# An attention block and two mixture-of-experts layers on one core: the first expert's row list and row evictions rearranged

## The chip, the cores and the metric

The kernel runs on one core of one Trainium2 chip. The metric is the device time of one execution in microseconds (us); lower is better. Five engines work on their own instruction streams, each in order: TensorE (PE in the profile, its weight loads PEld), VectorE (DVE), ScalarE (ACT), GpSimd (POOL) and SyncE (SP), which here only issues DMAs. Semaphores tie them together. On-chip memory is SBUF; TensorE writes to PSUM.

## The reference, cut to what matters

Attention over 4 batches, 8 heads, 768 positions in chunks of 32 gives `x`, 3072 rows of 512. Then come two layers of 8 experts with `relu(x @ w1[e]) @ w2[e]`:

```python
# layer 1: greedy assignment, each token to one expert, each expert takes 3072/8 = 384 tokens
logits = x @ w_gate
for idx in np.argsort(-logits.flatten()):
    tok, e = idx // E, idx % E
    if assigned[tok] >= 0 or counts[e] >= cap: continue
    assigned[tok] = e; counts[e] += 1
out[mask_e] = relu(x[mask_e] @ w1[e]) @ w2[e]
# layer 2: top 2 of 8 of noisy logits, weighted sum of the two experts
out[mask] += top2_w[mask, k, None] * (relu(x[mask] @ w1[e]) @ w2[e])
```

The change lies between attention and the first expert of layer 1.

## The kernel before, in words

**Attention** (`attention`) works on 24 tiles of 128 tokens and stores each row to DRAM (`xr`) as two f16 halves, high and low part, plus some columns of metadata. Constants are converted on POOL during attention, two of `ctx.chores` per tile (`setup`).

**Layer 1's assignment** (`route`) is done expert by expert: k = 0 to 7 are turns, and in each turn one expert fills up. A turn first proposes for each token its best open expert (`propose`: V, eq, mx, OH), then searches the threshold in several steps (GE on VectorE, counts on TensorE, `rps`), then names the expert (`m8`, and `est`, which the weight loads on SP's queue read) and the tokens that are sure. The second turn (k = 1) waits at line 782 before it starts on its steps.

**The list** (`lists1`, `slot_list`) turns a mask of tokens into a list of row numbers: each token's slot number is split into low bits (`bi`, 32 values) and high bits (`ai`, 12 values); `oa` is a one-hot of the high bits, `r` is `oa` times the token's number, `oh` (in the trace `sloh`) a one-hot of the low bits, [tokens of a partition 24, 32], made in steps of 512 elements. 24 small products with `oh[:, c]` as weights and `r[:, c]` as moving operand (`slps`) give the list in PSUM, 32 partitions x 12. Four evictions on VectorE (`idx`) lay it out on 128 partitions.

**The gather** (`gather1`) issues three indirect DMAs on POOL for the 384 rows of an expert. For experts 0 and 1, `transpose` transposes each tile of 128 rows on TensorE into one PSUM tile (`tps`, 8 blocks of 128, f16; the pool has two buffers), and one ScalarE operation evicts it to `xT`. For the others a transposing DMA does it. Then come `mm1` (products `m`) and for experts 0 to 4 `mm2_f32` (products `m2f`).

**The order of the instructions** is not left to the engines: the program keeps its own books (class `Pipe`) of when each engine would be free and each tile ready, and runs some twenty generators (loads, lists, gathers, splits of weights, routing) that each yield the time, in the books, at which their next instructions are due. TensorE's clock in the books drives them. While TensorE has nothing due, `until` writes one small product on ones (a filler, in the trace `m<-ones`) into its queue and advances the clock by its book time, 128 / 2.4 + 3 = 56.3 ns. What is written stays written: on the chip each engine runs its queue in order.

The weights of an expert are split into a high and a low f16 part (`split`, `halves`): the high part on ScalarE, the residual `w_..l` on VectorE or, for expert 0, also on POOL when it is idle in the books. The second turn's start (lines 778 to 783) asks for expert 0's first pair of `w1` tiles.

The lines of the books that matter here (`account`, 123 to 135, and `wait`, 195); `e` is the engine, `g` POOL:

```python
        elif e == "v":
            rate = 0.52 if op in ("tensor_scalar", "tensor_copy") and not ps else 6.25 if op == "reciprocal" else 1.04
            cost = 69.0 + 60.0 * ptr + rate * n
        elif e == "s":
            cost = (51.0 if ps else 93.0) + 94.0 * (ptr or "accum_out" in kw) + 0.833 * n
        else:
            cost = 147.0 + 1.887 * n if op == "tensor_tensor" else (245.0 if ptr else 122.0) + 0.832 * n

        if op in ("tensor_tensor", "scalar_tensor_tensor") and not ps:
            if e == "g":
                if self.t["v"] > start:
                    start += 200.0
                    self.t["v"] += cost
...
        self.until(lambda: self.rdy("p", *aps) <= self.t["p"] + 60.0, spare)
```

`ps` says that an operand lies in PSUM, `n` is the number of elements in a partition, `rdy` adds about 0.2 us for the way from engine to engine. `mm1` calls `pipe.wait(*w1, xT, spare=ps)` (line 1205) ahead of an expert's first product.

Of the kernel before, what the change touches and what calls it, by code (L numbers as in the profile page):

```python
# [9 lines left out]
F16 = mybir.dt.float16  # L10
BF16 = mybir.dt.bfloat16
I32 = mybir.dt.int32
AF = mybir.ActivationFunctionType
ALU = mybir.AluOpType
# [10 lines left out]
NTOK, DM, E, FF = B * S, H * D, 8, 1024  # L25
KT, FT = DM // 128, FF // 128
G = NTOK // 128
# [585 lines left out]
def slot_list(ctx, pi, na, low, ids, late=0.0):  # L613

    pipe, pool = ctx.pipe, ctx.rt
    V_, P_ = pipe.V, pipe.P
    ni, nc_ = ids.shape[2], ids.shape[1]  # L620

    def tl(n, shape, dt):
        return pool.tile(shape, dt, tag=f"sl{n}", name=f"sl{n}")

    bi, ai = (tl(n, [128, nc_], I32) for n in ("bi", "ai"))
    V_.tensor_scalar(bi, pi, low - 1, None, op0=ALU.bitwise_and)
    V_.tensor_scalar(ai, pi, low.bit_length() - 1, None, op0=ALU.arith_shift_right)
    yield pipe.t["v"] - 100
    oa = tl("oa", [128, nc_, na], F16)
    V_.tensor_tensor(  # L630
        oa, ai.unsqueeze(2).to_broadcast([128, nc_, na]),
        ctx.cols[low][:, :na].unsqueeze(1).to_broadcast([128, nc_, na]), op=ALU.is_equal,
    )
    yield pipe.t["v"] - 100
    r = tl("r", [128, nc_, na, ni], F16)
    V_.tensor_tensor(
        r, oa.unsqueeze(3).to_broadcast([128, nc_, na, ni]), ids.unsqueeze(2).to_broadcast([128, nc_, na, ni]),
        op=ALU.mult,
    )
    oh = tl("oh", [128, nc_, low], F16)  # L640
    step = 512 // low
    for c in range(0, nc_, step):
        yield pipe.t["v"] - 100
        cs = slice(c, min(c + step, nc_))
        m = cs.stop - cs.start
        V_.tensor_tensor(
            oh[:, cs], ctx.iota16[:, :low].unsqueeze(1).to_broadcast([128, m, low]),
            bi[:, cs].unsqueeze(2).to_broadcast([128, m, low]), op=ALU.is_equal,
        )
    ctx.spread += 1  # L650
    yield pipe.rdy("p", oh, r) + late
    yield from lock(ctx)
    ps = ctx.ms.tile([low, na, ni], F32, tag="msl", name="slps")
    for c in range(nc_):
        P_.matmul(
            ps.rearrange("p a b -> p (a b)"), oh[:, c], r[:, c].rearrange("p a b -> p (a b)"),
            start=(c == 0), stop=(c == nc_ - 1),
        )
    yield pipe.rdy("v", ps) - (0 if late else 200)
    return ps  # L660


def lists1(ctx):

    pipe, pool = ctx.pipe, ctx.rt
    V_ = pipe.V
    for k in range(E):
        yield lambda: k in ctx.sure
        mk = ctx.sure[k]
        ps = yield from positions(ctx, mk.unsqueeze(1), "l1")  # L670
        yield lambda: k in ctx.closed
        pos = ps[:, 0]
        if ctx.closed[k] is not None:
            at, before = ctx.closed[k]
            pos = pool.tile([128, G], F32, tag="lpos", name=f"lpos{k}")
            V_.tensor_tensor(pos, ps[:, 0], before, op=ALU.add)
            V_.tensor_tensor(mk, mk, at, op=ALU.add)
        na = CAP // 128
        pi = pool.tile([128, G], I32, tag="slpi", name="slpi")
        V_.scalar_tensor_tensor(pi, mk, -FAR, pos, op0=ALU.mult, op1=ALU.add)  # L680
        unlock(ctx)
        ps = yield from slot_list(ctx, pi, 4 * na, 32, ctx.tokid)
        for q in range(4):
            V_.tensor_scalar(
                ctx.idx1[32 * q : 32 * q + 32, k], ps[:, :, 0].rearrange("p (a q) -> p q a", q=4)[:, q],
                float(NTOK // 2), None, op0=ALU.add,
            )
        unlock(ctx)
        ctx.listed.add(k)


def route(ctx):
# [7 lines left out]
    pipe, pool = ctx.pipe, ctx.rt  # L700
    V_, P_ = pipe.V, pipe.P
# [27 lines left out]
    for k in range(E):  # L729
        def tl(shape, dt, n, **kw):  # L730
            return pool.tile(shape, dt, tag="rt" + n, name=f"{n}_{k}", **kw)
# [7 lines left out]
        def est():  # L739
            V_.tensor_scalar(ctx.est[:, k : k + 1], m8[:1], -1.0, float(E), op0=ALU.mult, op1=ALU.add)  # L740
            ctx.est_known.add(k)
# [36 lines left out]
        if k:  # L778
            s0, cand = 0, ctx.cand0
            if k == 1:  # L780

                yield lambda: k - 1 in ctx.listed and 0 in ctx.W and ctx.W[0]["w1"]
            *_, (V, OH, mx) = prop
        else:
            s0 = 2
            V, OH, mx = ctx.V0, ctx.OH0, ctx.mx0
            dg = pst([128, E])
            P_.matmul(dg, ctx.onesb[:NH], ctx.flh, start=True, stop=True)
            dgh = tl([128, E], F32, "dgh")
            V_.tensor_copy(dgh, dg)  # L790
            dg = dgh
            tables = top(dg, plan.shifts[1], slice(off[1], off[2]), slice(off[2], off[-1] + 1))
            next(tables)
            next(tables)
            cand = R[:, off[1] :].bitcast(F32)
        for s in range(s0, NS):
            nj, o = plan.nj[s], off[s]
            GE = tl([128, G * NJ], F16, "GE")[:, : G * nj].rearrange("p (c j) -> p c j", j=nj)
            step = G if k else G // 2
# [90 lines left out]
        V_.scalar_tensor_tensor(fl8, score, smax, ctx.e8f, op0=ALU.is_equal, op1=ALU.mult)  # L890
        V_.tensor_scalar(above, V, tf, None, op0=ALU.is_gt)
        V_.tensor_reduce(m8, fl8, axis=AX.X, op=ALU.max)
        inc, exc = tl([128, G], F32, "inc"), tl([128, G], F16, "exc")
        ind, bE = tl([128, E], F32, "ind"), tl([128, E], F32, "bE")
        cs, slack = tl([128, E], F32, "cs"), tl([128, E], F32, "slack")
# [4 lines left out]
        for i in range(0, G, G // 4):  # L900
            P_.matmul(cg, ctx.ones16, NQ[:, :, i : i + G // 4], start=(i == 0), stop=(i == G - G // 4))
        V_.scalar_tensor_tensor(at, mx, m8, at, op0=ALU.is_equal, op1=ALU.mult)
        est()
        V_.tensor_scalar(bE, ctx.e8f, m8, -2.0 * BIG, op0=ALU.is_equal, op1=ALU.mult)
        V_.tensor_tensor_scan(inc, ctx.keep[:, 0], at, 0.0, op0=ALU.mult, op1=ALU.add)
        V_.tensor_reduce(cs, cg, axis=AX.X, op=ALU.add)
# [373 lines left out]
    return ps  # L1280


def transpose(ctx, xT, rows, tile_):

    pipe = ctx.pipe
    yield pipe.rdy("p", tile_)
    ps = ctx.m2.tile([128, 2 * KT, 128], F16, tag="m2", name="tps")
    for kt in range(2 * KT):
        pipe.P.transpose(ps[:, kt], rows[:, 128 * kt : 128 * kt + 128], ctx.id16)
    pipe.S.activation(xT, ps, AF.Copy)  # L1290


def gather1(ctx, k):
# [5 lines left out]
    xg = []  # L1299
# [14 lines left out]
    for a in range(NA):  # L1314
        rows = xg[a][:, :DM].bitcast(F16)
        if k > 1:
            yield pipe.rdy("y", xg[a])
            pipe.D.dma_start_transpose(xT[:, :, 128 * a : 128 * a + 128], rows)
        else:
            yield from transpose(ctx, xT[:, :, 128 * a : 128 * a + 128], rows, xg[a])  # L1320
    ctx.X1[k] = (xT, ix)
    for a in range(NA):
        pipe.G.tensor_copy(ix[:, a : a + 1], xg[a][:, DM : DM + 1])
# [558 lines left out]
def setup(ctx, cp):  # L1882
# [9 lines left out]
    def half(n, src, dt=F16):  # L1892
        tl = cp.tile(list(src.shape), dt, name=n)
        nc.gpsimd.tensor_copy(tl, src)
        setattr(ctx, n, tl)
# [48 lines left out]
    def cols(low):  # L1944
        half(f"cols{low}", getattr(ctx, f"cols{low}"))
        ctx.cols[low] = getattr(ctx, f"cols{low}")


    ctx.chores = [
        lambda: half("e8", ctx.e8f),  # L1950
        lambda: half("tri16", ctx.tri),
        lambda: half("iota16", ctx.iota),
        lambda: half("tokid", ctx.tokid),
        lambda: half("slotid", ctx.slotid),
        lambda: cols(32),
# [67 lines left out]
```

## Time and profile before

| | |
|---|---|
| time, median of 3 runs | 1055.89 us (1055.35 to 1056.14) |
| the profiled execution | 1053.0 us, its span 1051.2 us |
| busy PE / DVE / ACT / POOL | 986.2 / 642.3 / 461.8 / 296.0 us |
| mean granted TensorE clock | 0.976 |
| end of attention, first turn of routing, list | up to 152.6 us |
| first gather issued | 152.87 us |
| first product of expert 0 | 162.45 us |

Times in rows are microseconds from the start of the span. A row of a timeline has start, duration, engine, line, operation, output <- inputs, shape and count, and in square brackets the idle time ahead of it with what ended it. Line 68 is that of a helper through which all instructions behind attention pass, so rows are told apart by their tiles.

### The profile page before, as it was taken

How to read it: one execution, taken by the hardware profiler on the slowest of the kernel's cores; microseconds unless marked ns; L12 is line 12 of the kernel's file. 1: busy time of each engine (PE TensorE's matmuls, PEld its weight loads, DVE VectorE, ACT ScalarE, POOL GpSimd, SP SyncE). 2: the span in 40 equal slices, each digit the busy share in tenths (PEclk: the TensorE clock that was granted, in tenths of full speed). 3: DMA queues.
4: the chain of work that ended last, by engine and by line, in shares of the span. 5: the costliest groups of instructions: out<-in, count | busy, mean ns of one | idle time of the engine just before them, and what ended most of it. 6: DMA issues, size and time to landing. Idle time of an engine off the chain costs nothing.

```text
span 1051.2 us, 21987 instructions
## 1 busy us (share of the span) xinstructions
PE 986.2 (94%) x8312; PEld 592.7 (56%) x8312; DVE 642.3 (61%) x2096; ACT 461.8 (44%) x817; POOL 296.0 (28%) x471
## 2 busy tenths in 40 slices
PE   7787649999999999998989999999999999999997
PEld 4676546767676676544555454455555555555553
DVE  6687775666666758695774846545455454564221
ACT  2576514444534446986506535245153351533110
POOL 6565414101102023101021323333233331232321
PEclk9899859999999999999999999999999999999999
DMA  8898833557578486959349748539367393664520
GB/s 238 255 267 235 304 137 123 186 159 210 169 225 203 151 203 192 305 165 201 62 105 268 241 133 244 140 106 260 95 203 176 88 286 87 167 116 110 115 66 31
DMA packets 147253, 184.61 MB, mean 176 GB/s; under 512 B 105558, under 2 KB 106070, under 8 KB 145608
## 3 DMA queue, kind: packets, MB, share of 16 engines
q1 hardware_dynamic: 129814, 131.74, 46.2%
q0 software_dynamic: 13872, 45.15, 14.7%
q10 hardware_dynamic: 3458, 6.30, 1.7%
q8 instruction: 66, 1.08, 0.5%
q14 instruction: 43, 0.35, 0.1%
HBM read 127.10 MB, written 32.44 MB: 152 GB/s over the span
## 4 chain that ended last, share of the span: by engine, by line
PE 71%; DMA 11%; DVE 6%; issue 5%; ACT 3%; SPq 2%; POOL 1%; ACTq 0%; POOLq 0%; DVEq 0%
PE m L68 55%; PE m2f L68 10%; DMA v<-vctx_dram 4%; PE rps L68 3%; DMA k<-kT_dram 1%; DMA yT<-rb 1%; SPq L280 1%; DMA xg<-xr,idx 1%; ACT junk L68 1%; SPq L278 1%; DMA xr<-rb 1%; PE slps L68 1%; PE sb L304 1%; DVE sloh L68 1%; DMA st<-x_dram 1%
## 5 line engine op out<-in xcount | busy, mean ns | idle before, releaser
L68 PEld LDWEIGHTS <-hT 128*128 128x128 f16 (+2 forms) x1800 | 143.5, 99 | 159.5 <-issue 5.1
L68 ACT ACTIVATE hT<-m 128x384 f16<-128x384 f32 (+2 forms) x152 | 75.6, 499 | 274.6 <-PE m L68 271.6
L68 DVE SCALAR_TENSOR_TENSOR hT<-m,hT 128x384 f16<-128x384 f32 (+2 forms) x152 | 86.4, 569 | 96.3 <-ACT hT L68 96.2
L68 ACT ACTIVATE junk<-st 128x1024 f16<-128x1024 f32 x108 | 113.6, 1052 | 61.4 <-DMA st<-x_dram 26.0
L68 PE MATMUL m2f<-st,hT 128*128 128x256 f32 x480 | 127.6, 398 | 0.6 <-ACT hT L68 0.6
L68 POOL DMA_INDIRECT out_dram<-pv,ts x47 | 48.9, 1040 | 257.5 <-DVE pv L68 99.3
L68 DVE SCALAR_TENSOR_TENSOR pv<-m,ys,pv 128x512 f32<-128x512 f32 (+2 forms) x47 | 33.5, 714 | 118.8 <-PE m L68 118.7
L68 PE MATMUL m<-xT,w_0h 128*128 128x384 f16 (+2 forms) x384 | 96.6, 331 | 2.8 <-DMA xT<-xg 2.8
L68 PE MATMUL m<-xT,w_2h 128*128 128x384 f16 (+2 forms) x384 | 96.7, 331 | 1.7 <-DVE hT L68 1.7
L68 PE MATMUL m<-xT,w_1h 128*128 128x384 f16 (+2 forms) x384 | 96.5, 331 | 0.0
L68 PE MATMUL m<-xT,w_3h 128*128 128x384 f16 (+2 forms) x384 | 96.4, 331 | 0.0
L68 PEld LDWEIGHTS m2f<-st,hT 128*128 128x128 f32 x480 | 83.4, 190 | 10.2 <-ACT hT L68 1.0
L68 PE MATMUL m<-w_3h,hT 128*128 128x512 f16 (+2 forms) x300 | 71.6, 345 | 1.4 <-DVE hT L68 1.4
L68 PE MATMUL m<-w_0h,hT 128*128 128x512 f16 (+2 forms) x300 | 72.7, 348 | 0.0
L68 PE MATMUL m<-w_1h,hT 128*128 128x512 f16 (+2 forms) x300 | 72.1, 347 | 0.0
L68 PE MATMUL m<-w_2h,hT 128*128 128x512 f16 (+2 forms) x300 | 71.5, 345 | 0.0
L68 PE MATMUL m<-xT,w_2l 128*128 128x384 f16 (+2 forms) x192 | 63.6, 331 | 0.0
L68 PE MATMUL m<-xT,w_1l 128*128 128x384 f16 (+2 forms) x192 | 63.6, 331 | 0.0
L68 PE MATMUL m<-xT,w_3l 128*128 128x384 f16 (+2 forms) x192 | 63.6, 331 | 0.0
L68 PE MATMUL m<-xT,w_0l 128*128 128x384 f16 (+2 forms) x192 | 63.6, 331 | 0.0
L68 POOL DMA_INDIRECT xg<-x,rows x54 | 53.2, 985 | 29.9 <-issue 11.7
L68 POOL DMA_INDIRECT xg<-xr,idx x24 | 25.0, 1040 | 129.1 <-DVE idx L68 39.0
(336 smaller groups left out, 1870.2 us busy)
## 6 DMA issues: line engine op xcount, KB each, us to landing
st<-w_dram SPq DMA_DIRECT2D x64, 512.0 KB
st<-x_dram SPq DMA_DIRECT2D x64, 512.0 KB
xr<-rb SPq DMA_DIRECT2D x24, 264.0 KB
x<-rb SPq DMA_DIRECT2D x24, 264.0 KB
v<-vctx_dram SPq DMA_DIRECT2D x12, 520.0 KB
v<-vctx_dram SPq DMA_DIRECT2D x24, 260.0 KB
q<-qT_dram SPq DMA_DIRECT2D x12, 512.0 KB
out_dram<-zero ACTq DMA_DIRECT2D x24, 256.0 KB
```

The costliest lines, as they stand in the source:

```text
L68: return f(*args, **kw)
L278: nc.sync.dma_start(behind[:, n : n + 1], flown[-AHEAD])
L280: nc.sync.dma_start(out, src)
L304: nc.tensor.matmul(sc[CH * c : CH * c + CH, hp], q[:, hp, CH * o : CH * o + CH], k[:, :, hp, k0 : k0 + KEYS], start=True, stop=True,)
```

## The change

- In `slot_list` with 32 low values, the low bits are converted to f16 (`bw`, then a copy), the one-hot becomes [32, 24], tokens innermost, in one operation against a new constant `ctx.lows`, and the weights of product c are `oh[:, :, c]`. This holds for the eight lists of layer 1.
- `lows` is one more chore on POOL, in fourth place.
- In `lists1`, for the first expert, index evictions 1 and 3 of four go to ScalarE.
- In `route`, `est` of the first turn is written directly behind `m8` instead of behind the products that follow; the second turn waits for expert 0's gathers to be issued instead of for its list.
- `transpose` for expert 0 evicts the first half of the columns on ScalarE and the second on VectorE.

```diff
@@ slot_list
-    bi, ai = (tl(n, [128, nc_], I32) for n in ("bi", "ai"))
-    V_.tensor_scalar(bi, pi, low - 1, None, op0=ALU.bitwise_and)
-    V_.tensor_scalar(ai, pi, low.bit_length() - 1, None, op0=ALU.arith_shift_right)
+    bi, ai = tl("bi", [128, nc_], F16 if low < 128 else I32), tl("ai", [128, nc_], I32)
+    if low < 128:
+        bw = tl("bw", [128, nc_], I32)
+        V_.tensor_scalar(bw, pi, low - 1, None, op0=ALU.bitwise_and)
+        V_.tensor_scalar(ai, pi, low.bit_length() - 1, None, op0=ALU.arith_shift_right)
+        V_.tensor_copy(bi, bw)
...
-    oh = tl("oh", [128, nc_, low], F16)
+    if low < 128:
+        yield pipe.t["v"] - 100
+        oh = tl("oh", [128, low, nc_], F16)
+        V_.tensor_tensor(oh, ctx.lows, bi.unsqueeze(1).to_broadcast([128, low, nc_]), op=ALU.is_equal)
+        hot = lambda c: oh[:, :, c]
+    else:
+        oh = tl("oh", [128, nc_, low], F16)
+        hot = lambda c: oh[:, c]
...
-            ps.rearrange("p a b -> p (a b)"), oh[:, c], r[:, c].rearrange("p a b -> p (a b)"),
+            ps.rearrange("p a b -> p (a b)"), hot(c), r[:, c].rearrange("p a b -> p (a b)"),
@@ lists1
-            V_.tensor_scalar(
-                ctx.idx1[32 * q : 32 * q + 32, k], ps[:, :, 0].rearrange("p (a q) -> p q a", q=4)[:, q],
-                float(NTOK // 2), None, op0=ALU.add,
-            )
+            out, src = ctx.idx1[32 * q : 32 * q + 32, k], ps[:, :, 0].rearrange("p (a q) -> p q a", q=4)[:, q]
+            if k or q % 2 == 0:
+                V_.tensor_scalar(out, src, float(NTOK // 2), None, op0=ALU.add)
+            else:
+                pipe.S.activation(out, src, AF.Copy, bias=float(NTOK // 2))
@@ route
-                yield lambda: k - 1 in ctx.listed and 0 in ctx.W and ctx.W[0]["w1"]
+                yield lambda: 0 in ctx.gathered and 0 in ctx.W and ctx.W[0]["w1"]
...
         V_.tensor_reduce(m8, fl8, axis=AX.X, op=ALU.max)
+        if not k:
+            est()
...
         V_.scalar_tensor_tensor(at, mx, m8, at, op0=ALU.is_equal, op1=ALU.mult)
-        est()
+        if k:
+            est()
@@ transpose, called with first = not k
+    if first:
+        pipe.S.activation(xT[:, :KT], ps[:, :KT], AF.Copy)
+        pipe.V.tensor_copy(xT[:, KT:], ps[:, KT:])
+        return
     pipe.S.activation(xT, ps, AF.Copy)
@@ setup
+    def lows():
+        ctx.lows = cp.tile([128, 32, G], F16, name="lows")
+        nc.gpsimd.tensor_copy(ctx.lows, ctx.iota[:, :32].unsqueeze(2).to_broadcast([128, 32, G]))
         lambda: half("iota16", ctx.iota),
+        lows,
```

## Rows read from the trace of the kernel before

**Rows 1.** The page: busy time, and a group (busy, mean ns | idle before).

```profile
PE 986.2 (94%) x8312; PEld 592.7 (56%) x8312; DVE 642.3 (61%) x2096; ACT 461.8 (44%) x817; POOL 296.0 (28%) x471
...
L68 DVE SCALAR_TENSOR_TENSOR pv<-m,ys,pv 128x512 f32<-128x512 f32 (+2 forms) x47 | 33.5, 714 | 118.8 <-PE m L68 118.7
```

**Rows 2.** Stretches: length, busy PE, PEld, DVE, ACT, POOL, clock, DMA share, GB/s.

```profile
162.45:200.20 37.75, 37.74 (x356) 25.55 (x353) 24.58 (x103) 13.33 (x23) 9.40 (x9) 1.00 0.41 147
200.20:202.10 1.90, 0.06 (x1) 0.06 (x2) 0.40 (x2) 0.00 (x0) 0.05 (x1) 1.00 0.77 298
...
400.00:425.00 25.00, 23.28 (x178) 13.83 (x177) 21.91 (x69) 21.51 (x37) 11.59 (x26) 1.00 0.83 235
...
450.00:500.00 50.00, 44.49 (x279) 23.03 (x278) 38.03 (x126) 37.92 (x65) 7.12 (x17) 0.97 0.82 189
...
525.00:575.00 50.00, 46.43 (x338) 25.94 (x336) 34.30 (x106) 17.71 (x30) 12.23 (x12) 1.00 0.67 177
575.00:1025.00 450.00, 449.87 (x2847) 237.57 (x2845) 231.36 (x610) 163.07 (x260) 136.71 (x137) 1.00 0.58 156
```

**Rows 3.** Timeline of VectorE, the first expert's list: one-hot and index evictions.

```profile
150.35 1.02 DVE L68 TENSOR_TENSOR sloh<-iota,slbi 128x512 f16<-128x512 f16 x2
151.94 0.65 DVE L68 TENSOR_SCALAR idx<-slps 32x3 int32<-32x3 f32 x4 [0.56 <-PE slps L68]
```

**Rows 4.** Timeline of POOL, the first gather's issue.

```profile
152.87 1.18 POOL L68 DMA_INDIRECT xg<-xr,idx  x1 [19.66 <-DVE idx L68]
```

**Rows 5.** Timeline of TensorE, 151 to 162.5 us, lines left out.

```profile
151.09 0.81 PE L68 MATMUL slps<-slr,sloh 128*32 128x12 f16 x24 [2.69 <-DVE sloh L68]
...
158.22 0.62 PE L68 MATMUL tps<-id,xg 128*128 128x128 f16 x8 [0.23 <-DMA xg<-xr,idx]
...
160.50 0.61 PE L68 MATMUL tps<-id,xg 128*128 128x128 f16 x8
161.04 0.80 PE L68 MATMUL rps<-OH,GE 128*15 128x8 f16 x24
161.77 0.84 PE L68 MATMUL m<-ones 128*128 128x128 f16 x12
162.45 0.33 PE L68 MATMUL m<-xT,w_0h 128*128 128x384 f16 x1
```

**Rows 6.** Timeline of ScalarE, 151 to 162.2 us, lines left out.

```profile
151.07 1.06 ACT L68 ACTIVATE junk<-st 128x1024 f16<-128x1024 f32 x1 [24.26 <-DVE sloh L68]
...
152.55 1.06 ACT L68 ACTIVATE junk<-st 128x1024 f16<-128x1024 f32 x1 [0.34 <-DMA st<-w_dram]
...
160.09 2.08 ACT L68 ACTIVATE xT<-tps 128x1024 f16<-128x1024 f16 x2 [0.19 <-PE tps L68]
```

**Rows 7.** Timeline of VectorE, two operations of 192 f16 elements.

```profile
193.65 0.36 DVE L68 TENSOR_TENSOR eq<-eq,e 128x192 f16<-128x192 f16 x1
...
194.57 0.26 DVE L68 TENSOR_TENSOR OH<-eq,mx 128x192 f16<-128x192 f16 x1
```

**Rows 8.** Timeline of VectorE, the second routing's start.

```profile
154.88 1.40 DVE L68 SCALAR_TENSOR_TENSOR w_0l<-st,s,w_0h 128x512 f16<-128x512 f32 x2
156.20 0.61 DVE L68 TENSOR_REDUCE V<-L 128x24 f32<-128x192 f32 x1
...
159.49 0.56 DVE L68 TENSOR_TENSOR GE<-V,c_consts_dram 128x360 f16<-128x360 f32 x1
```

**Rows 9.** Groups of POOL, 0 to 131 us: busy, mean ns | idle before.

```profile
L387 POOL TENSOR_TENSOR rb<-x,rb 128x512 f16<-128x512 f32 x22 | 25.5, 1161 | 1.8
...
L382 POOL COPY rb<-ixs 128x1 f32<-128x1 f32 x24 | 10.1, 422 | 45.5 <-DVE ixs L217 45.5
```

**Rows 10.** Timelines around expert 1's gather: VectorE, POOL, TensorE.

```profile
195.40 0.64 DVE L68 TENSOR_SCALAR idx<-slps 32x3 int32<-32x3 f32 x4
...
196.32 1.05 POOL L68 DMA_INDIRECT xg<-xr,idx  x1 [19.34 <-DVE idx L68]
...
202.04 0.62 PE L68 MATMUL tps<-id,xg 128*128 128x128 f16 x8 [1.85 <-DMA xg<-xr,idx]
```

More of the change, by code (lines that the diff above doesn't have):

```diff
@@ L623, in tl @@
         return pool.tile(shape, dt, tag=f"sl{n}", name=f"sl{n}")
-    bi, ai = (tl(n, [128, nc_], I32) for n in ("bi", "ai"))
-    V_.tensor_scalar(bi, pi, low - 1, None, op0=ALU.bitwise_and)
-    V_.tensor_scalar(ai, pi, low.bit_length() - 1, None, op0=ALU.arith_shift_right)
+    bi, ai = tl("bi", [128, nc_], F16 if low < 128 else I32), tl("ai", [128, nc_], I32)
[5 more added lines that the diff above has]
+    else:
+        V_.tensor_scalar(bi, pi, low - 1, None, op0=ALU.bitwise_and)
+        V_.tensor_scalar(ai, pi, low.bit_length() - 1, None, op0=ALU.arith_shift_right)
     yield pipe.t["v"] - 100
@@ L639, in slot_list @@
     )
-    oh = tl("oh", [128, nc_, low], F16)
+    if low < 128:
[6 more added lines that the diff above has]
+        hot = lambda c: oh[:, c]
     step = 512 // low
-    for c in range(0, nc_, step):
+    for c in range(0, nc_ if low == 128 else 0, step):
         yield pipe.t["v"] - 100
@@ L683, in lists1 @@
         for q in range(4):
-            V_.tensor_scalar(
-                ctx.idx1[32 * q : 32 * q + 32, k], ps[:, :, 0].rearrange("p (a q) -> p q a", q=4)[:, q],
-                float(NTOK // 2), None, op0=ALU.add,
-            )
+            out, src = ctx.idx1[32 * q : 32 * q + 32, k], ps[:, :, 0].rearrange("p (a q) -> p q a", q=4)[:, q]
+            if k or q % 2 == 0:
+                V_.tensor_scalar(out, src, float(NTOK // 2), None, op0=ALU.add)
+            else:
+                pipe.S.activation(out, src, AF.Copy, bias=float(NTOK // 2))
         unlock(ctx)
@@ L1280, in mm2_f32, with transpose @@
     return ps
-def transpose(ctx, xT, rows, tile_):
+def transpose(ctx, xT, rows, tile_, first=False):
     pipe = ctx.pipe
@@ L1319, in gather1 @@
         else:
-            yield from transpose(ctx, xT[:, :, 128 * a : 128 * a + 128], rows, xg[a])
+            yield from transpose(ctx, xT[:, :, 128 * a : 128 * a + 128], rows, xg[a], not k)
     ctx.X1[k] = (xT, ix)
```

## The prediction

> **What bounds the kernel now.** I read the shares of the page first: TensorE is busy 94% of the span [rows 1]. The table by stretches then shows where it is not: it is gapless from 162.45 to 200.2 us, idle 1.84 us of the 1.90 behind that, and gapless to 0.13 us from 575 to 1025 [rows 2]. So whatever moves the first product of expert 0 (162.45), or the hole at 200, moves the end by about as much, except where the transition between the layers takes it up or adds to it: three stretches there hold 1.72 + 5.51 + 3.57 = 10.8 us of idle [rows 2]. What the change touches lies ahead of 162.45 and, for the one-hot, also ahead of the hole at 200. Third, I read the timeline of each engine up to 162.45 and ask which wait ends last there.
>
> The chain: one-hot on VectorE to 151.37, 24 list products on TensorE from 151.09 to 151.90, four index evictions to 152.59 [rows 3, 5], first gather issued at 152.87 [rows 4], its transposes 5.3 us behind the issue at 158.22, the third tile's at 160.50 [rows 5], the evictions of tiles two and three on ScalarE to 162.17 [rows 6], first product. But TensorE shows almost no idle there (0.23 us ahead of 158.22): where nothing is due it runs products on ones, 12 of them right ahead of 162.45 [rows 5]. These fillers are written into TensorE's in-order queue when the program is made: `pipe.wait` adds one at a time until the planner's books say that the rows are there. **So a real gain ahead of the first product counts only if the books see it too, and a delay that only the books see costs real time.** My forecast hangs on that step.
>
> **The parts.**
>
> *One-hot.* Two operations, 1.02 us [rows 3], become one of 768 elements, all operands 16 bit and tokens innermost. The price is read from two rows of 192 elements: 0.36 us where an operand repeats along the innermost axis, 0.26 where tokens are innermost [rows 7]. The 0.10 between them is 192 x 0.52 ns, so at 1.04 and 0.52 ns an element both leave 0.16 us fixed; 768 x 0.52 + 160 = 0.56 us, 0.46 less. Against that stands the copy of the low bits to f16: between 0 (slack of the short operations around it) and 0.17 (the pitch of the short index evictions, 0.65 for four [rows 3]); I take 0.10. At expert 0 the first 16 list products started behind the first half (151.09); now all wait for the whole, 150.35 + 0.56 + 0.06 = 150.97: a gain of 0.12, less up to 0.10.
>
> *Weights of the list products* are now read with a stride of 24 elements. No row shows a strided weight load. Nearest: 24 products whose 8 moving columns are strided last 0.80 us, 24 with 12 contiguous ones 0.81 [rows 5]. I take 0; the upper end is a rival below.
>
> *Index evictions.* Four at a pitch of 0.167 us end at 152.59 [rows 3]. Two stay on VectorE (0.33 less). The other two stand in ScalarE's queue behind the square sums of the first weight tile, which run from 151.07 to 152.13 and have an accumulator read behind them [rows 6]; then two of 0.1 to 0.2: 152.4 to 152.6, or 152.75 if the four take turns, since they read one bank. Behind them on ScalarE wait the next square sums (152.55 [rows 6]), on POOL the gathers. So the gathers move by -0.2 to +0.2; I take 0.
>
> *est* goes ahead by one short VectorE operation (an index eviction shows what one takes, 0.16). The weight loads on SP's queue start that much earlier; they feed ScalarE's and VectorE's split, which isn't the last wait. 0.
>
> *The second routing's condition.* Before, it waits for list 0 and for expert 0's first weight quarter. In the trace it begins (V<-L, 156.20) directly behind the two residuals of that quarter (154.88, 1.40 us) [rows 8], 3.3 us behind the first gather's issue. The new condition, gathers issued, is then long true, and the weight condition stays. This edit moves nothing: 0.
>
> *The lows constant* is one more POOL operation of 768 elements during attention, where POOL's waits for VectorE sum to 45.5 us [rows 9]; the chores behind it move by one place. 0, and about 1.2 us if that cover is gone (a two-input POOL operation of 512 lasts 1.16 [rows 9]).
>
> *Row evictions.* ScalarE's 1.02 us for 1024 columns becomes 0.5 to 0.6 for 512. VectorE's half, 512 columns out of PSUM, lies between 0.43 (0.16 + 512 x 0.52 ns, from above) and 0.71 (a two-input operation on 512 PSUM columns, the pv line [rows 1]); I take 0.6. But VectorE is in order, and its queue holds the second routing's start, V to GE, until 160.05 [rows 8]. Tile one could be evicted from 158.85; its VectorE half runs from 160.05 to 160.65. The transposes' PSUM pool has two buffers, so the third tile's transposes wait for it: 160.7 instead of 160.50. **The gain of splitting is lost to the queue: +0.2.**
>
> *Fillers.* The planner's books (Pipe.account) are arithmetic inside the program; I use them for order and count only. For the kernel before they come to: GE ends at 28.95 us of the books, POOL's subtraction for w_1l pushes VectorE's clock by 147 + 1.887 x 512 = 1113 ns to 30.07; the last rows are ready through ScalarE at 30.53; TensorE's clock is 29.82 behind the routing's 24 products; 12 fillers of 56.3 ns bring it to within the 60 ns that `wait` allows. The trace has exactly 12 [rows 5]. After: VectorE's clock is about 29.98 (0.09 less from est and list), and three copies of 69 + 1.04 x 512 = 601 ns queue behind it to 31.78, ready for TensorE at 31.98. TensorE's clock behind the third transposes, one filler and the 24 products is 29.68; (31.92 - 29.68) / 0.0563 = 40 fillers. That makes 41 in place of 12. In the trace a filler takes (162.45 - 161.77) / 12 = 0.057 us: 29 x 0.057 = 1.65 us. The real rows will be there at 161.9 to 162.5; TensorE runs fillers until about 164.3.
>
> **First product:** 162.45 + 0.2 + 1.65 = 164.3, +1.85.
>
> *Expert 1.* Its one-hot, the third routing's start and its index evictions stand in one unbroken run on VectorE that ends at 196.04; the gather is issued at 196.32, and TensorE waits 1.85 us for it until 202.04 [rows 10]. One-hot 0.46 less, copy 0.10 more: against TensorE's stream the gather comes 0.36 earlier, and the hole shrinks by that. The other six lists save VectorE time that nothing waits for.
>
> **Sum:** 0.2 + 1.65 - 0.36 = +1.5 us. Against the profiled execution (1053.0 us around a span of 1051.2, and 2.9 below the median of the three runs) that is 1054.5; against the median, 1055.9 + 1.5 = **1057.4 us**. The own range of this case: the filler term between 1.1 and 1.9 (20 to 33 fillers), and of the transition's 10.8 us I let a seventh move either way (1.5): 1055.4 to 1059.2.
>
> **The rivals.**
>
> *The copies run when the rows come.* If they get ahead of the routing's start (its weight condition is met later than I read), each tile is evicted in 0.6 us, with 12 fillers or fewer: third transposes at 160.4, rows at 161.6, first product at 161.6 to 161.9. That is -0.7, with expert 1 -1.0: 1054.9. For it: ScalarE's evictions of tiles two and three last 2.08 us and end last now [rows 6]. Against it: the order of [rows 8]. If the halves take turns, VectorE behind ScalarE, the first product comes at 162.2 and the end at 1055.3. The Trainium skill, page "PSUM — Partial Sum Buffer", section "PSUM bank collisions raise a hardware error", speaks for turns: reads of one bank and quadrant by two engines have to be kept apart, ScalarE and VectorE too. No row of before shows such a pair.
>
> *The strided weight loads are slow.* 24 list products take 0.81 us, 0.033 each [rows 5]. If the stride doubles that, each list costs 0.8 us more on TensorE, eight times, 6.4 us: with the forecast's steps 1063. It decides from about 0.01 us a load on (1.9 us in all). Against it: the strided moving columns above. The Trainium skill, page "Advanced Engine Details and Errata", section "SBUF Cachelines", states that a stream which touches another 16-byte line with each access is slower; these loads are 48 bytes apart. It gives no figure.
>
> *The transition gives time back.* The shift re-draws the order of VectorE, ScalarE and SP between the layers; if that closes half of the 10.8 us there, 1057.4 - 5.4 = 1052. No row favours it.
>
> **How the numbers follow.** 0.2% is 2.1 us, about what a measurement of this kernel tells from no change: faster ends at 1053.8, slower begins at 1058.0. Forecast 0.6 (0.38 of it within, 0.22 slower), copies in time 0.2 (0.14 within, 0.05 faster, 0.01 slower), strided loads 0.1 (slower), transition 0.1 (0.08 faster, 0.02 within). Faster 0.13, same 0.54, slower 0.33. The range takes in the forecast's own, the first rival, and small doses of the other two: 1054.0 to 1060.0.
>
> **What would show it.** Right: some 41 fillers behind the last transposes, a first product near 164.3 with the rows there 2 us earlier; VectorE's three copies directly behind GE; sloh near 0.56 us; the hole at expert 1 near 1.5 us; V<-L still right behind w_0l. Wrong: 12 fillers; copies ahead of V<-L; list products of 24 that last over 1 us; or a first product at 164.3 with an end that doesn't follow.

## The result and the profile after

The changed kernel takes 1072.08 us (median of 5 runs, 1066.93 to 1075.64) beside 1056.14 for the kernel before (median of 5): ratio 1.0134, 95% interval 1.0098 to 1.0171, by that ratio 14 us more. The forecast was 1.5 us more, and the range ended at 1060.0. Its profiled execution took 1069.25 us with a span of 1067.5, the one of before 1053.0 and 1051.2.

The page of after, against [rows 1], says who pays: TensorE is busy 15.4 us longer with 37 products more, all of them fillers (29 ahead of expert 0, 29 ahead of expert 2, less the 21 that before has in the transition); VectorE is busy 3.4 us shorter.

```profile
PE 1001.6 (94%) x8349; PEld 606.0 (57%) x8349; DVE 638.9 (60%) x2097; ACT 460.7 (43%) x819; POOL 300.0 (28%) x472
```

**The list and the first product.** These are the timelines of after up to expert 0's first product: TensorE, then VectorE and ScalarE, with lines left out (start, duration, engine, line, operation, tiles, shape, count, and in brackets the idle time ahead).

```profile
149.12 1.80 PE L68 MATMUL slps<-slr,sloh 128*32 128x12 f16 x24 [2.56 <-DVE sloh L68]
...
159.50 0.61 PE L68 MATMUL tps<-id,xg 128*128 128x128 f16 x8 [0.41 <-DVE xT L68]
159.94 0.22 PE L68 MATMUL m<-ones 128*128 128x128 f16 x1
160.09 0.79 PE L68 MATMUL rps<-OH,GE 128*15 128x8 f16 x24
160.81 1.46 PE L68 MATMUL m<-ones 128*128 128x128 f16 x23
162.11 0.17 PE L68 MATMUL tot<-sq,onesb 128*128 128x1 bf16 x1
162.14 1.11 PE L68 MATMUL m<-ones 128*128 128x128 f16 x17
163.08 0.49 PE L68 MATMUL m<-xT,w_0h 128*128 128x384 f16 x2
```

```profile
148.51 0.55 DVE L68 TENSOR_TENSOR sloh<-lows,slbi 128x768 f16<-128x768 f16 x1
150.95 0.15 DVE L68 TENSOR_SCALAR idx<-slps 32x3 int32<-32x3 f32 x1 [1.89 <-PE slps L68]
151.33 0.15 DVE L68 TENSOR_SCALAR idx<-slps 32x3 int32<-32x3 f32 x1 [0.23 <-ACT idx L68]
...
155.25 0.61 DVE L68 TENSOR_REDUCE V<-L 128x24 f32<-128x192 f32 x1
...
158.55 0.56 DVE L68 TENSOR_TENSOR GE<-V,c_consts_dram 128x360 f16<-128x360 f32 x1
159.03 0.74 DVE L68 COPY xT<-tps 128x512 f16<-128x512 f16 x2
160.77 0.43 DVE L68 COPY xT<-tps 128x512 f16<-128x512 f16 x1 [0.99 <-ACT xT L68]
...
151.13 0.16 ACT L68 ACTIVATE idx<-slps 32x3 int32<-32x3 f32 x1 [1.01 <-DVE idx L68]
151.51 0.16 ACT L68 ACTIVATE idx<-slps 32x3 int32<-32x3 f32 x1 [0.22 <-DVE idx L68]
...
160.14 0.60 ACT L68 ACTIVATE xT<-tps 128x512 f16<-128x512 f16 x1 [0.97 <-PE tps L68]
```

The first row is the news. The 24 list products last 1.80 us in place of 0.81 [rows 5], 0.075 us each. All list products together, in the groups of TensorE from the first one-hot on, first of after, then of before:

```profile
L68 PE MATMUL slps<-slr,sloh 128*32 128x12 f16 (+4 forms) x399 | 20.9, 191 | 2.6 <-DVE sloh L68 2.6
```

```profile
L68 PE MATMUL slps<-slr,sloh 128*32 128x12 f16 (+4 forms) x399 | 12.7, 170 | 2.7 <-DVE sloh L68 2.7
```

That is 8.2 us on TensorE, 1.03 for each of the eight lists. The second thing to see is the 1 + 23 + 17 = 41 fillers that the prediction counted: the last copy ends at 161.20, TensorE runs fillers to 163.08.

**Where the rest arises.** The stretches of after that answer to those of [rows 2] where TensorE was idle or that come last (length, busy PE, PEld, DVE, ACT, POOL, clock, DMA share, GB/s):

```profile
200.20:202.10 1.90, 1.90 (x16) 1.43 (x16) 0.44 (x3) 0.00 (x0) 0.95 (x1) 1.00 0.93 259
400.00:425.00 25.00, 22.79 (x159) 15.82 (x158) 18.40 (x88) 17.45 (x32) 5.22 (x10) 0.98 0.36 116
450.00:500.00 50.00, 44.81 (x304) 24.49 (x303) 39.03 (x128) 40.17 (x74) 7.76 (x22) 0.93 0.68 198
525.00:575.00 50.00, 45.37 (x325) 24.98 (x324) 33.53 (x116) 11.22 (x24) 11.98 (x11) 1.00 0.55 159
575.00:1025.00 450.00, 446.34 (x2812) 234.49 (x2810) 234.90 (x617) 169.75 (x267) 136.37 (x133) 1.00 0.58 156
```

The hole at 200 us is gone, the three stretches of the transition hold 2.21 + 5.19 + 4.63 = 12.0 us of idle instead of 10.8, and the last stretch 3.7 instead of 0.13. (The stretches are the same times of the clock, and after is up to 19 us late in them, so they don't hold quite the same work.) The start of the first one-hot differs from execution to execution (147.4 to 153.4 us in the sixteen traces of this case), whatever the kernel, so I put the stages on one scale: start of an expert's first product less the start of the first one-hot, and of that the difference to the kernel before. Each number is worked out from two rows of the timelines of either kernel.

| us later than before | expert 0 | 1 | 2 | 5 | 7 | layer 2's first | end |
|---|---|---|---|---|---|---|---|
| after | 2.5 | 0.8 | 3.7 | 9.8 | 18.9 | 13.5 | 18.1 |
| before_lows (order of before) | -0.4 | -0.5 | -0.5 | -0.5 | -0.5 | -3.4 | -2.1 |
| after_pairs | 2.3 | -0.5 | 1.3 | 2.4 | 8.9 | 3.5 | 6.3 |
| after_nosplit | -0.1 | -0.2 | 1.2 | 8.6 | 11.2 | 6.0 | 7.5 |
| before_strided2 | 0.0 | 0.3 | 2.8 | 5.4 | 7.2 | 1.8 | 2.7 |
| before_split | 2.6 | 0.1 | 1.8 | 4.1 | 3.4 | 0.0 | 6.2 |
| before_booked | 1.7 | -0.6 | 1.3 | 3.6 | 2.8 | 1.5 | 13.1 |
| pairs_unbooked | -0.4 | -2.6 | -2.4 | -1.1 | -0.3 | -5.5 | -2.7 |

The names are those of the experiments below. The second row has the order of the kernel before and, up to expert 7, its times to half a microsecond; in the transition, where transfers end last, it is 3 us off. So up to expert 7 one trace tells a microsecond, behind it only the medians do. In the last two columns the chip counts too: from layer 2's first product to the end before_strided, which has the order of before, falls back 8.7 us on the chip of before_split, and rest_unbooked 3.6 on that of before_booked, while the eight traces of the two other chips lie between -1.3 and +2.8.

### The profile page after: what moved, and what is told of

Same layout as the page of the kernel before. It is cut to its first block, busy times and chain, and to the rows that moved or that the text cites. A ratio compares the mean times of both kernels' runs of the same rounds, so it can differ in the third digit from the quotient of the medians.

```text
span 1067.5 us, 22062 instructions
## 1 busy us (share of the span) xinstructions
PE 1001.6 (94%) x8349; PEld 606.0 (57%) x8349; DVE 638.9 (60%) x2097; ACT 460.7 (43%) x819; POOL 300.0 (28%) x472
## 4 chain that ended last, share of the span: by engine, by line
PE 77%; DMA 9%; DVE 7%; issue 3%; SPq 2%; ACT 2%; POOL 0%; ACTq 0%; POOLq 0%; DVEq 0%
PE m L68 59%; PE m2f L68 11%; PE rps L68 3%; DMA v<-vctx_dram 3%; DMA k<-kT_dram 2%; PE slps L68 2%; SPq L280 1%; SPq L278 1%; DMA c_wg<-wg_dram 1%; DMA st<-x_dram 1%; DMA q<-qT_dram 1%; DMA c_consts_dram<-consts_dram 1%; DVE hT L68 1%; DMA out_dram<-pv,ts 1%; DVE sloh L68 0%
## 5 line engine op out<-in xcount | busy, mean ns | idle before, releaser
L68 PEld LDWEIGHTS m2f<-st,hT 128*128 128x128 f32 x480 | 84.5, 191 | 10.8 <-ACT hT L68 1.3
L68 POOL DMA_INDIRECT xg<-x,rows x54 | 55.5, 1028 | 24.2 <-issue 13.6
L68 POOL DMA_INDIRECT pv<-out_dram,tg x47 | 45.8, 975 | 53.4 <-DMA out_dram<-pv,ts 30.5
```

The lines of the kernel that those rows point to most:

```text
L68: return f(*args, **kw)
```

## The experiments

The theory: two parts of the change cost the time, the strided weight loads (A) and the split of the row evictions, by way of the planner's books. The rival (B): the loads lie beside other work, and the new order of all that follows is the loss. Ratios stand against runs of the kernel before on the same chip. The experiments ran on four chips, where its medians were 1057.7 us (after_dense, before_strided, strides, before_split), 1049.6 (after_pairs, before_strided2, after_nosplit, pairs_nosplit), 1049.8 (before_fill, before_lows, pairs_unbooked, before_rest) and 1055.4 (before_booked, rest_unbooked).

| | ratio to before | 95% |
|---|---|---|
| after (the change) | 1.0134 | 1.0098 to 1.0171 |
| after_dense | 1.0247 | 1.0187 to 1.0307 |
| before_strided | 1.0175 | 1.0126 to 1.0224 |
| before_split | 1.0056 | 1.0015 to 1.0097 |
| before_strided2 | 1.0061 | 1.0036 to 1.0086 |
| after_pairs | 1.0078 | 1.0055 to 1.0101 |
| after_nosplit | 1.0089 | 1.0054 to 1.0125 |
| pairs_nosplit | 1.0049 | 1.0018 to 1.0080 |
| before_fill | 1.0026 | 1.0006 to 1.0047 |
| before_lows | 1.0003 | 0.9987 to 1.0019 |
| pairs_unbooked | 1.0009 | 0.9993 to 1.0025 |
| before_rest | 0.9979 | 0.9959 to 1.0000 |
| before_booked | 1.0061 | 1.0030 to 1.0093 |
| rest_unbooked | 0.9962 | 0.9934 to 0.9990 |

### Two runs that changed more than they should

To move the stride from TensorE's read to VectorE's write, and the other way round, without touching the order:

```diff
 after_dense, in the kernel after
-        oh = tl("oh", [128, low, nc_], F16)
-        V_.tensor_tensor(oh, ctx.lows, ...)
-        hot = lambda c: oh[:, :, c]
+        oh = tl("oh", [128, nc_, low], F16)
+        V_.tensor_tensor(oh.rearrange("p c l -> p l c"), ctx.lows, ...)
+        hot = lambda c: oh[:, c]
 before_strided, in the kernel before
-    oh = tl("oh", [128, nc_, low], F16)
+    oh = tl("oh", [128, low, nc_], F16).rearrange("p l c -> p c l")
```

> The kernel after, instruction for instruction in the same order, but the one operation writes its result with the low values innermost (VectorE writes with a stride of 64 bytes), so that TensorE loads each list product's weights contiguously. Theory A (the strided weight loads carry about half of the loss): a list of 24 products of layer 1 falls from 1.79 us to about 0.77 us, eight lists give back 8 us, and the time is 1064 us (1063 to 1066; the one-hot itself may go from 0.55 to 0.96 us, 0.4 us at each of the first two experts). Theory B (the loss is the new order of the instructions and the fillers; the loads are hidden): 1072 us, whatever the list products do.

> The kernel before, same order of instructions, with one edit: the one-hot tile is laid out with tokens innermost and the two operations write through a transposed view, so that the list products load weights 48 bytes apart. Theory A: the lists take 1.8 us instead of 0.76 to 0.81, the time is 1056 + 8.2 = 1064 us (1062.5 to 1066). Theory B: 1056 to 1057 us.

Measured: +2.5% and +1.8%, beyond both theories. The lists did what A said (0.76 to 0.81 us in after_dense, 1.8 to 1.9 in before_strided), but the one-hot became the trouble (in before_strided, writing 48 bytes apart, its first two operations take 3.67 us, not 1.02); VectorE in after_dense:

```profile
151.67 3.50 DVE L68 TENSOR_TENSOR sloh<-lows,slbi 128x768 f16<-128x768 f16 x1
```

The same 768 elements with a write that jumps 64 bytes from one element to the next take 3.50 us, not 0.55. So neither run tells A from B; they show a second price of the same stride, on the writer's side.

### What a weight load costs by its stride

The kernel after, the one-hot stored in groups of S tokens, S = 1, 2, 3, 4, 6, 8, 12, 24 for the eight lists:

```diff
+        S = (1, 2, 3, 4, 6, 8, 12, 24)[ctx.spread % 8]
+        oh = tl("oh", [128, nc_ // S, low, S], F16)
...
-        hot = lambda c: oh[:, :, c]
+        hot = lambda c: oh[:, c // S, :, c % S]
```

> The kernel after, same order of instructions, with another stride of the one-hot's weights for each of the eight lists: 2, 4, 6, 8, 12, 16, 24 and 48 bytes. What a load costs by its stride. If what counts is the number of 16-byte lines that a load touches, a list takes 0.77 us at 2 bytes, rises to 1.8 us at 16 bytes and is the same 1.8 us at 24 and 48. If any stride over one element is slow, 4 bytes already takes 1.8 us. If cost goes by distance, 16 bytes takes about 1.1 us and only 48 bytes 1.8. If loads are not slow but something else in the kernel after makes these lists slow (theory B), all eight take 1.8 us. Time by the first: about 1067 us.

The eight lists on TensorE and the eight one-hots on VectorE, in this order of strides (2, 4, 6, 8, 12, 16, 24, 48 bytes):

```profile
155.10 0.81 PE L68 MATMUL slps<-slr,sloh 128*32 128x12 f16 x24 [5.50 <-DVE sloh L68]
199.60 0.76 PE L68 MATMUL slps<-slr,sloh 128*32 128x12 f16 x24
249.12 0.77 PE L68 MATMUL slps<-slr,sloh 128*32 128x12 f16 x24
288.55 0.96 PE L68 MATMUL slps<-slr,sloh 128*32 128x12 f16 x24
327.49 1.28 PE L68 MATMUL slps<-slr,sloh 128*32 128x12 f16 x24
373.36 1.61 PE L68 MATMUL slps<-slr,sloh 128*32 128x12 f16 x24
415.52 1.55 PE L68 MATMUL slps<-slr,sloh 128*32 128x12 f16 x24
425.89 1.79 PE L68 MATMUL slps<-slr,sloh 128*32 128x12 f16 x24
...
151.56 3.49 DVE L68 TENSOR_TENSOR sloh<-lows,slbi 128x768 f16<-128x768 f16 x1
198.29 0.82 DVE L68 TENSOR_TENSOR sloh<-lows,slbi 128x768 f16<-128x768 f16 x1
246.39 1.50 DVE L68 TENSOR_TENSOR sloh<-lows,slbi 128x768 f16<-128x768 f16 x1
285.00 0.55 DVE L68 TENSOR_TENSOR sloh<-lows,slbi 128x768 f16<-128x768 f16 x1
```

Up to 6 bytes the stride is free, from 8 to 16 bytes the list grows in step with it, behind that it changes little. The Trainium skill, page "Advanced Engine Details and Errata", section "SBUF Cachelines", lets a stream run at full rate while accesses fall on the same 16-byte line; the bend at 16 bytes agrees, the free 4 and 6 bytes too, as the list products themselves need about (0.77 - 0.17) / 23 = 0.026 us each (0.17 is what one small product alone shows) and can hide a load that is no longer. The rise at 8 bytes, where two weights still share a line, doesn't follow from that sentence. At 48 bytes the 24 loads take 1.70 us in the records of weight loads, 0.071 each. Of what was expected, counting lines comes nearest, but the step isn't sharp: 8 bytes already cost, and 48 cost more than 16. The single run took 1070.72 us.

### The loads and the split, each alone

```diff
 before_strided2: each of the two operations stores its own tokens innermost
+            part = oh[:, cs].rearrange("p c l -> p (c l)").rearrange("p (l c) -> p l c", c=m)
+            V_.tensor_tensor(part, iota by low, bi by token, op=ALU.is_equal)
 before_split, in the kernel before
-            yield from transpose(ctx, ..., rows, xg[a])
+            yield from transpose(ctx, ..., rows, xg[a], not k)    # halves, as after
 after_pairs, in the kernel after: 4 bytes apart, written in the order of storage
+        oh = tl("oh", [128, nc_ // 2, low, 2], F16)
 after_nosplit, in the kernel after;  pairs_nosplit: this and after_pairs
-            yield from transpose(ctx, ..., rows, xg[a], not k)
+            yield from transpose(ctx, ..., rows, xg[a])
```

> The kernel before, same order of instructions; each of the two one-hot operations stores its tokens innermost (16 tokens in the first, 8 in the second), in the order of storage, so VectorE writes without a stride (1.02 us as before) and TensorE loads 16 weights of each list 32 bytes apart and 8 of them 16 bytes apart. By the eight strides (1.61 us at 16 bytes, 1.55 at 24, 1.79 at 48) a list takes 1.6 to 1.7 us, 0.85 more than before. Theory A: + 0.85 x 8 = 6.8 us, ratio 1.005 to 1.008. Theory C: the loss grows or shrinks behind the lists: ratio above 1.011 or below 1.003. Theory B (loads are hidden): 1.000.

> The kernel after, same order of instructions; the one-hot is still one operation, laid out in pairs of tokens (12 pairs, 32 low values, 2 tokens) and written in the order of storage, so that weights are 4 bytes apart, a stride at which the run with eight strides showed 0.76 us for a list. The operation: 0.55 us if VectorE keeps its rate with 2 elements innermost, 0.82 to 0.96 if not. Theory A (eight slow lists and the split eviction's new order add up): 8.2 us less than the kernel after, that is before + 6 us, ratio 1.004 to 1.008. Theory C (the slow lists also shift what is late in the transition, so that their loss isn't one for one): ratio below 1.003 or above 1.010.

> The kernel before with one edit: the first expert's transposed rows are evicted in halves by ScalarE and VectorE. The written order then has 27 fillers more ahead of the first product, 29 ahead of expert 2's products where there were none, and 59 instead of 21 in the transition. Theory A (the split costs fillers and little else): first product +1.8 us, the hole of 1.85 us at expert 1 perhaps closed, 29 x 0.057 = 1.65 us at expert 2, 38 x 0.057 = 2.2 us in the transition unless they lie in idle time: 1056 + 1.6 to 5.6, about 1059 us. Theory B (order and fillers are the whole loss): 1066 us or more.

> The kernel after with ScalarE alone evicting the first expert's transposed rows, as before; the strided loads stay. The written order has 92 fillers ahead of the first product (121 with the split), none at expert 2 (29), 47 in the transition (0). Theory A: the eight lists are left, + 8.2 us, less about 0.5 for the earlier lists, up to 1.5 more for the 26 fillers in the transition: ratio 1.007 to 1.009. If the split costs nothing and all of the loss is the loads' (theory D): ratio 1.013, as the kernel after.

> The kernel after with both suspects taken out: weights 4 bytes apart as in pairs, ScalarE alone evicts the transposed rows. What is left of the change: one one-hot operation, index evictions on two engines, est early, the second routing's condition, the constant. Theory A: nothing is left of the loss: 0.4 us gained at each of the first two lists, up to 1.5 us lost to fillers in the transition: ratio 0.998 to 1.002. If a third part of the change costs something (est, the condition, the evictions in turns): ratio above 1.003.

before_strided2 has VectorE's work and the order of before, and a list of it reads

```profile
193.58 1.63 PE L68 MATMUL slps<-slr,sloh 128*32 128x12 f16 x24
```

0.87 more than the 0.76 of the free strides, eight times 7.0; measured 0.0061 x 1050 = 6.4 us (3.8 to 9.0). Theory A's loads stand, about one for one, and B falls, as the order here is that of before. In the table above the delay grows to 7.2 at expert 7, 0.9 us a list on the mean. after_pairs and after_nosplit take one cause out of the change each, and each takes out part of the loss (1.0078 and 1.0089 of 1.0134). before_split costs 0.56% with contiguous loads, a little more than the 1059 us expected; beside the 27 more ahead of expert 0 it has fillers where the prediction had not looked, 29 ahead of expert 2's first product and 38 more between the first products of layer 2's first and second expert. TensorE of before_split ahead of expert 2:

```profile
263.95 1.46 PE L68 MATMUL m<-ones 128*128 128x128 f16 x23
265.24 0.30 PE L68 MATMUL rps<-OH,GE 128*120 128x64 f16 x3
265.38 0.50 PE L68 MATMUL m<-ones 128*128 128x128 f16 x6
265.72 0.33 PE L68 MATMUL m<-xT,w_0h 128*128 128x384 f16 x1
```

pairs_nosplit missed: 1.0049 where 0.998 to 1.002 was expected. A third part seemed left.

### Is it the split, or what the books make of it?

```diff
 pairs_unbooked, in after_pairs: the copy is made, VectorE's clock and the rows' time aren't moved
+        t = pipe.t["v"]
         pipe.V.tensor_copy(xT[:, KT:], ps[:, KT:])
+        pipe.t["v"] = t
+        pipe.ready[xT.tensor.name] = (pipe.t["s"], "s")
 before_booked, in before_split: the copy is booked and not made; ScalarE evicts all
-        pipe.V.tensor_copy(xT[:, KT:], ps[:, KT:])
+        pipe.account("v", "tensor_copy", (xT[:, KT:], ps[:, KT:]), {})
 before_fill, in the kernel before, for experts 0 and 2
+                for _ in range(29):
+                    (product on ones, not booked)
```

> The kernel after with weights 4 bytes apart, and with VectorE's three copies out of the books (VectorE's clock isn't moved, the rows count as ready when ScalarE's half is). The split itself stays on the chip. The written order has 84 fillers ahead of the first product (121 after, 92 before), 10 at expert 2, 47 in the transition. Theory A (the books cost the time, not the split): the first product comes 13.1 to 13.7 us behind the start of the one-hot less 2.5, that is within 0.5 us of where the kernel before has it (12.1), and the ratio is 0.998 to 1.003. Theory H (VectorE's queue and the turns at the PSUM bank make the split itself late): first product 13.5 us or more behind the one-hot, TensorE idle ahead of it, ratio 1.005 or more.

> The kernel before_split, every engine's instructions in the same order, but the split itself isn't done: ScalarE evicts the whole of each transposed tile, while the books are charged as if VectorE had taken half (119, 29 and 59 fillers as there). Theory J (what the split costs is what the books make of it): ratio 1.003 to 1.008, as before_split with 1.0056. Theory H (VectorE's queue and the turns at the PSUM bank on the chip): 0.999 to 1.002.

> The kernel before, same order of instructions, with 29 fillers more ahead of expert 0's first product and 29 ahead of expert 2's: the fillers that the split eviction added ahead of the transition, without its new order. Theory E (fillers pay their 1.65 us each, the hole of 1.85 us at expert 1 takes the first group back): expert 0 starts 1.65 us later, expert 1 about 0, expert 2 and all behind it + 1.65 us, ratio 1.001 to 1.003; what the split costs beyond that, some 4 us, is then the order that it draws in the transition. Theory F (fillers are all that the split costs): ratio 1.005 to 1.007.

First TensorE of before_booked, then of pairs_unbooked, around the first product:

```profile
157.52 0.61 PE L68 MATMUL tps<-id,xg 128*128 128x128 f16 x8
159.04 1.51 PE L68 MATMUL m<-ones 128*128 128x128 f16 x24
160.42 1.00 PE L68 MATMUL m<-ones 128*128 128x128 f16 x15
161.25 0.49 PE L68 MATMUL m<-xT,w_0h 128*128 128x384 f16 x2
```

```profile
162.38 0.61 PE L68 MATMUL tps<-id,xg 128*128 128x128 f16 x8 [0.62 <-DVE xT L68]
162.82 0.22 PE L68 MATMUL m<-ones 128*128 128x128 f16 x1
163.70 0.34 PE L68 MATMUL m<-ones 128*128 128x128 f16 x3
163.88 0.58 PE L68 MATMUL m<-xT,w_0h 128*128 128x384 f16 x2
```

before_booked does nothing that the kernel before doesn't do, except that its books believe in three copies; it costs 0.61%, as much as before_split (0.56%). pairs_unbooked makes the copies, waits for them (0.62 us ahead of the third transposes) and costs 0.09%, within what can be told from nothing. So what the split costs is what the books make of it, to within the intervals of some 0.3%. Of its 6 us in the kernel before, before_fill gives 0.26%, 2.7 us (0.6 to 4.9), to 58 fillers (2 x 29 x 0.057 = 3.3, less what the hole at expert 1 takes). The 38 further fillers ahead of layer 2's second expert come to 38 x 0.057 = 2.2 us, and there before_split falls back 2.4 us and before_booked 2.2. Behind that before_split falls back 3.8 more, but so does before_strided on the same chip, by 7.7, with the order of before; of before_booked's 9.4 rest_unbooked loses 4.6 on the same chip, and the rest stays open.

In the change itself the second half is another one, as after has no fillers in layer 2. There it is a wait for hT ahead of expert 7. It lasts 5.0 us in the four traces with the order of after (after, after_dense, strides, after_pairs), whatever the loads; TensorE of after_pairs:

```profile
467.91 0.61 PE L68 MATMUL m<-w_3h,hT 128*128 128x512 f16 x1 [5.01 <-DVE hT L68]
```

In the twelve other traces no wait for hT at this place is over 1.5 us, before_split, after_nosplit and pairs_unbooked included, so it takes the booked copies and the rest of the change together. after_pairs is 3.0 us late at expert 6 and 8.9 at expert 7. What VectorE does in it stands below, under the transition.

### The small parts, and a version that is faster

```diff
 before_lows: the constant alone.  before_rest: index evictions on two engines, est early, the condition
 rest_unbooked: before_rest, and the split of the row evictions kept out of the books
```

> The kernel before, same order of instructions, with the constant of 768 elements added on POOL during attention, where nobody reads it. Theory A (it lies in POOL's waits): ratio 0.998 to 1.002. Theory G (it delays attention's end, and is the third part of the loss): 1.003 to 1.006.

> The kernel before with the small parts alone: the first list's index evictions on two engines, est of the first turn directly behind m8, the second routing's condition. One-hot, its loads and the row evictions as before. The written order has 92 fillers ahead of the first product as before, 3 at expert 2, none in the transition (21 before). Theory A (these parts move nothing): ratio 0.998 to 1.002. Theory I (one of them is the third part of the loss): 1.003 to 1.006.

> The small parts alone (before_rest, ratio 0.9979) and the split of the row evictions out of the books: the first product of expert 0 about as far behind the one-hot as before (pairs_unbooked: 0.36 us less), 84 fillers ahead of it, 10 at expert 2, none in the transition. If the split kept out of the books is worth its earlier rows: 0.995 to 0.998, better than both kernels. If it is worth nothing, as VectorE's queue holds the copies: 0.998 to 1.000.

The constant costs nothing (1.0003), the small parts don't either (0.9979). Both together with the one-operation one-hot in pairs gave 1.0049 in pairs_nosplit, but 1.0009 in pairs_unbooked, which holds all of them too. So no part is left that loses by itself; the 0.5% (5.1 us) of pairs_nosplit goes with its order. Its trace goes from 1.1 us early at expert 3 to 2.0 late at expert 5 and 2.8 at expert 7, and loses 1.2 more ahead of layer 2's second expert, where 47 fillers stand instead of 21; pairs_unbooked has the same 47 fillers, but is 0.3 us early at expert 7, as its order fills the hole at expert 1 (-2.6). What is late between experts 3 and 5 was not traced and stays open. So a redrawn order can move this kernel by some 0.4%.

rest_unbooked, the change without its one-hot and with the split out of the books, beats both kernels: 0.9962 (0.9934 to 0.9990), 4 us under the kernel before. That the split adds to it isn't shown: before_rest has 0.9979, the intervals overlap, and the first product of expert 0 comes 0.5 us earlier than before with the split and 0.4 without.

## Why the prediction was wrong

**Weights of the list products: the step that failed.** "Nearest: 24 products whose 8 moving columns are strided ... I take 0." The moving operand was no neighbour of the weights: there 8 columns are read, here 32 weights of each product, and a list went from 0.76 to 1.79 us. That row could not have shown a price, either: at the 0.071 us for 32 strided weights, 8 columns would take 0.071 x 8 / 32 = 0.018 us (an estimate), less than the 0.026 that a product needs anyway. The right answer stood among the rivals ("the strided weight loads are slow") at a chance of 0.1 and 6.4 us, 1063 in all; by rows it is 8.2, by before_strided2 at 16 and 32 bytes 6.4 of time. The cited rule on lines was set aside for a row that measured something else; no row measured a strided load, so it should have had more than a tenth.

**Fillers: the mechanism right, the size off.** 41 fillers were forecast and are there; from the third transposes to the first product it is 3.58 us instead of 1.95, + 1.63 against 1.65 forecast. But the books' delay was followed to the first product only; that is the second step that failed. The same shift wrote 29 more fillers ahead of expert 2's first product and drew, in the order of after, the wait of 5 us ahead of expert 7. By before_fill and before_booked the split costs 2.7 us in fillers and about 6 in all in the order of before, and taking it out of the books gains 0.69% in the change with pairs (1.0078 to 1.0009), 7 us, where the prediction had 1.85.

**Row evictions.** The order came as written: V behind w_0l, copies behind GE, the third transposes waiting for VectorE's copy. They start 10.99 us behind the one-hot, before 10.15; of these 0.84 some 0.2 was forecast, and the rest comes with VectorE's queue, which is late as a whole: GE starts 10.04 us behind the one-hot, before 9.14 [rows 3, 8]. The slow list isn't what makes it late, or not alone: with lists of 0.81 us GE starts at 9.85 in after_pairs and in before_split. Why it does was not traced. A copy takes 0.43 us, not 0.6: the lower of the two bounds, 0.16 + 512 x 0.52 ns, was right. The halves take turns: VectorE's third copy starts at 160.77, ScalarE's has ended at 160.14 + 0.60 = 160.74. The Trainium skill, page "PSUM — Partial Sum Buffer", section "PSUM bank collisions raise a hardware error", asks for such turns; here the rows show them for xT and for idx. They cost nothing at the third tile, as fillers cover them.

**First product:** + 2.5 us against + 1.85; the excess is the later third transposes. The slow list at the head of the chain makes the gather late (issued 3.45 us behind the one-hot, before 2.52), but not the first product: with the slow list and no split it is 0.1 us early (after_nosplit) or on time (before_strided2), with the split and a fast list 2.3 late (after_pairs) or 2.6 (before_split).

**One-hot:** 0.55 us, forecast 0.56. **Index evictions:** 150.95 to 151.67 in turns, 0.7 us as before; forecast no gain. **est, condition, constant:** nothing, as forecast (before_rest, before_lows).

**Expert 1.** The gather is issued 4.58 us behind its one-hot, 5.03 before: 0.45 earlier against 0.36 forecast, in spite of the slow list, since idx waits there for VectorE. But the hole of 1.85 us vanished for another reason: 32 products of expert 0 stand between list and transposes in the written order, 24 before, and they fill it. That gave back about as much as the first group of fillers took.

**The transition.** I let a seventh of its 10.8 us move. In after it holds 12.0 of idle, and one wait there costs in two ways. TensorE of after around it, then VectorE in it:

```profile
468.09 0.59 PE L68 MATMUL m<-w_3h,hT 128*128 128x512 f16 x2
...
474.67 0.61 PE L68 MATMUL m<-w_3h,hT 128*128 128x512 f16 x1 [5.02 <-DVE hT L68]
475.50 1.06 PE L68 MATMUL m<-w_0h,hT 128*128 128x512 f16 x2
...
472.38 1.41 DVE L68 SCALAR_TENSOR_TENSOR w_2l<-st,s,w_2h 128x512 f16<-128x512 f32 x2
...
474.06 0.55 DVE L68 SCALAR_TENSOR_TENSOR hT<-m,hT 128x384 f16<-128x384 f32 x1
```

VectorE's residual of hT stood behind three pairs of weight residuals, from 469.73 on (the last pair is shown); TensorE idled 5.02 us, and behind that two products took 1.06 us where two took 0.59 ahead of it. The stretch (same columns as above) says why: the granted clock fell from 2.4 to 1.2 GHz with the idle time, is 0.66 on the mean of the stretch and back at 1.00 from 480 on:

```profile
470.00:480.00 10.00, 5.33 (x24) 2.19 (x25) 8.17 (x26) 3.96 (x9) 0.00 (x0) 0.66 0.63 205
480.00:490.00 10.00, 10.00 (x67) 5.04 (x65) 9.48 (x44) 8.07 (x12) 1.74 (x6) 1.00 0.23 60
```

**Sum.** Taken out of the change one behind the other, the loads (after to after_pairs) bring it from + 1.34% to + 0.78%, and the books' three copies (after_pairs to pairs_unbooked) from there to + 0.09%: 1.25 of 1.34%, 13 of 14 us, each step good to some 0.3 or 0.4%. Measured alone in the kernel before: loads 8.2 by rows (6.4 at the smaller strides), split 6, small parts -2: 10 to 12 us of the 14 (10 to 18). How much of the 14 each of the two has is known no closer, as every edit also redraws the order.

## What to carry to other kernels

When a layout is changed to make the writer fast, price the reader by a run or a bound of its own: a row with 8 strided moving columns says nothing of 32 strided weights, and here pieces of 4 bytes would have been free for TensorE (0.76 us for a list) and 0.82 us for VectorE. Where a program plans its order with books, an edit costs what the books believe, all the way to the end of the program: run the edit with its booking and without, and the booking without the edit.

## What was not expected of the hardware

- A weight load of 32 f16 values is hidden up to 6 bytes of stride (a list of 24 takes 0.76 to 0.81 us); it takes 0.96 us at 8 bytes, 1.28 at 12, 1.61 at 16, 1.55 at 24, 1.79 at 48.
- VectorE's comparison of 768 f16 elements takes 0.55 us with 4 or more tokens innermost, 0.82 with 2 (0.81 to 0.83 in after_pairs, which writes in the order of storage, so there the run of 2 and not the jump sets it), 1.50 with 3, and 3.49 where each written element lies 64 bytes from the last.
- VectorE copies 512 f16 columns out of PSUM in 0.43 us, ScalarE in 0.60.
